# Block sums of x by VectorE out of PSUM, column tiles in the order 0, 3, 1, 4, 2, 5, and another first tile of seven products

## The chip, the cores and the metric

One core of a Trainium2 chip runs the whole program. The metric is the device time of one execution in microseconds (us). The kernel before was timed three times; the median counts.

## What is computed

Three layers follow each other: attention with a soft cap, a first feed-forward with a softmax-weighted unit and a layer norm, and a second feed-forward with a SiLU gate. All data are fp32.

```python
scores = cap * tanh(q @ k.T / sqrt(64) / cap)          # 2 batches, 12 heads, 448 positions, 64 wide
x = softmax(scores) @ v                                # 896 tokens, 768 wide
h = x @ w_in                                           # 768 -> 1024
e = exp(h - max(h)); solu = h * e / (sum(e) + 1e-9)
ln = (solu - mean) / sqrt(var + 1e-6) * g_ln
x = ln @ w_out                                         # 1024 -> 768: the "x" of this study
g = x @ w_gate                                         # 768 -> 1536
out = (g / (1 + exp(-g)) * (x @ w_val)) @ w_out2       # 1536 -> 768
```

## The kernel before, in words

Every fp32 product is made of three TensorE products of rounded parts: a number is split into `hi`, which ScalarE writes (`hi_act`, line 68), and `lo`, what is left, which VectorE subtracts (`lo_dve`, line 77). Each split so costs one ScalarE row and one VectorE row. The tiles read in the trace carry the names of the program: `x<-lA,wo` is a product of the layer-normed tokens with w_out, `g<-x,g` one of x with gate weights.

The second x is made transposed, in six column tiles `j` of 128 (`ff1_x2`, line 565), each for all 896 tokens. A tile is 384 tokens out of `lA` and 512 out of `lB`, eight fp32 steps each, in halves that alternate; the first two tiles have their last 512 tokens in two blocks of 256. Each block fills a PSUM bank; there are eight banks (tag "m"), handed out in turn. At the end of a block ScalarE and VectorE split the bank into `self.x2[j]`.

w_out arrives as 64-bit floats, 512 KB for half a tile (`load_w_out`, line 553). A half is turned into fp32 by one ScalarE row and four VectorE rows, scaled by g_ln in four ScalarE rows, and split by one row of either. So VectorE has ten rows of 512 numbers for each column tile besides the splits of x itself. TensorE needs the first half of w_out for the first half of a tile, and the second half for the second.

The second feed-forward takes w_gate and w_val in twelve column tiles `fc`. Tile 0 and tiles 7 to 11 are done directly (`ff2_gv`). Tiles 1 to 6 use seven block products in place of eight (`ff2_gv_seven`, line 677): gate and value of 128 columns, two halves of the 768 rows, two halves of the tokens. Four of the seven take block sums of x, the tensors T1 to T4; the others take x itself. The sums of weights S1 to S4 are made by `sum_steps` (line 646), S2 and S4 by one split into one tile.

The block sums of x are made while x runs. GpSimd adds `hi` and `lo` of a column tile back to fp32 (128x896) and subtracts blocks of 448 tokens (`x_sums`, line 628): 6 additions and 12 subtractions in the tile `xf`. During tile 0 of the second feed-forward `x_split` (line 640) splits the four sums of 1344 numbers into T, four ScalarE and four VectorE rows.

The rows of TensorE and of the attention stand in program order; ScalarE, VectorE and GpSimd rows of this part are put in order by a scheduler at build time, and each engine then runs its rows strictly in that order. DMAs are issued by SyncE; the raw weights have two buffers (tag "raw"), so a load starts when the last reader of the load before the last is done.

Of the kernel before, what the change touches and what calls it, by code (L numbers as in the profile page):

```python
# [5 lines left out]
F32 = mybir.dt.float32  # L6
# [4 lines left out]
AF = mybir.ActivationFunctionType  # L11
ALU = mybir.AluOpType
# [25 lines left out]
class Kernel:  # L38
# [526 lines left out]
    def ff1_x2(self, j, get, N, o):  # L565

        st = {}

        def part(a, z):
            def f():  # L570
                l, w = get(), self.wos[j]
                if a == 0:
                    st["ps"] = self.pt.tile([128, 512], F32, name=f"x2_{j}_{o}", tag="m")[:, :N]
                ps = st["ps"]
                for fc in range(a, z):
                    self.mm3(ps, (w[:, 0, fc, :], w[:, 1, fc, :]), (l[:, fc, 0, :], l[:, fc, 1, :]),
                             fc == 0, fc == self.K1 - 1)
                if z == self.K1:
                    hi, lo = self.x2[j][:, 0, o:o + N], self.x2[j][:, 1, o:o + N]
                    self.hi_act(hi, ps)  # L580
                    self.lo_dve(lo, ps, hi)
                    if o + N == 896 and j > 1:
                        for m in range(3) if j == 2 else (j,):
                            x = self.x2[m].bitcast(F32)
                            self.G.tensor_tensor(self.xf[:, m], x[:, 0], x[:, 1], op=ALU.add)
                        self.x_sums(j - 2)
            return (3 * (z - a) * N / 2400, f)

        c = self.K1 // 2
        return [part(0, c), part(c, self.K1)]  # L590
# [34 lines left out]
            self.V.tensor_tensor(self.S1f[:, k], self.S1f[:, k], sg[:, :self.HN], op=ALU.add)  # L625
        self.split((self.A22 if o else self.A11 if first else self.A12)[k], sg)

    def x_sums(self, i):

        c = i - 1  # L630
        x = [self.xf[:, k + 3 * (m // 2), 448 * (m % 2):448 * (m % 2) + 448] for m in range(4) for k in range(3)]
        x = [x[3 * m:3 * m + 3] for m in range(4)]
        if i == 0:
            todo = [(0, 1, 0, k) for k in range(3)]
        else:
            todo = [(1, 3, 1, c), (3, 3, 0, c), (2, 2, 3, c)]
        for d, p, m, k in todo:
            self.G.tensor_tensor(x[d][k], x[p][k], x[m][k], op=ALU.subtract)

    def x_split(self, i):  # L640

        d = (0, 3, 1, 2)[i]
        src = self.xf[:, 3 * (d // 2):3 * (d // 2) + 3, 448 * (d % 2):448 * (d % 2) + 448]
        self.split([self.T[i][:, u] for u in range(2)], src)

    def sum_steps(self, fc):

# [29 lines left out]
    def ff2_gv_seven(self, fc):  # L677

        V, add, mult = self.V, ALU.add, ALU.mult
        n, k, ee = self.HN, fc % self.KD, self.ee  # L680
        a, s24, s31, a22 = self.gvs[fc]
        half = lambda t, h: t.rearrange("p (h u k f) -> p h u k f", h=2, u=2, k=3)[:, h]
        A11, A12, S2, S4, S3, S1 = (half(t, h) for t in (a, s24, s31) for h in range(2))
        A22 = a22.rearrange("p u (k f) -> p u k f", k=3)
        X = lambda kh, th: [[self.x2[3 * kh + c][:, u, 448 * th:448 * th + 448] for u in range(2)] for c in range(3)]
        T1, T2, T3, T4 = ([[t[:, u, c] for u in range(2)] for c in range(3)] for t in self.T)
        bank = lambda m: self.pt.tile([128, 512], F32, name=f"{m}_{fc}", tag="m")[:, :448]

        def product(acc, w, x, start):
            for c in range(3):  # L690
                self.mm3(acc, (w[:, 0, c], w[:, 1, c]), x[c], start and c == 0, c == 2, not start)

        sg, c22, p1, u2 = (ee[:, 448 * m:448 * m + 448] for m in range(4))
        last = fc == self.KD
        first, second, third = (lambda: None,) * 3 if last else self.sum_steps(fc + 1)
        if last:
            self.load_gv(fc + 1, 1)
        a = bank("g")
        product(a, A11, X(0, 0), True)
        self.A.activation(p1, a, AF.Copy)  # L700
        b = bank("b")
        product(b, S2, T2, True)
        V.tensor_tensor(u2, p1, b, op=add)
        product(a, A12, X(1, 0), False)
        self.A.activation(sg, a, AF.Silu)
        first()
        product(b, S3, T3, False)
        V.tensor_tensor(p1, p1, b, op=add)
        c = bank("c")
        product(c, S1, T1, True)  # L710
        V.tensor_tensor(c22, p1, c, op=add)
        second()
        if last:
            self.load_gv(fc + 1, 0)
        e = bank("e")
        product(e, A22, T4, True)
        V.tensor_tensor(p1, p1, e, op=add)
        third()
        product(c, S4, X(1, 1), False)
        V.tensor_tensor(u2, u2, c, op=add)  # L720
        self.A.activation(u2, u2, AF.Silu)
        G = self.G
        if last:
            V.tensor_tensor(p1, p1, sg, op=mult)
            V.tensor_tensor(c22, c22, u2, op=mult)
            self.split(self.A12[k], p1[:, :n])
            V.tensor_tensor(self.S1f[:, k, :64], self.S1f[:, k, :64], p1[:, n:], op=add)
            V.tensor_tensor(self.S1f[:, k, 64:], self.S1f[:, k, 64:], c22[:, :320], op=add)
            for w, src in ((slice(0, 64), p1[:, n:]), (slice(64, 512), c22)):
                self.split([p[:, w] for p in self.A22[k]], src)  # L730
            return
        V.tensor_tensor(self.S3f[:, k], p1[:, :n], sg[:, :n], op=mult)
        V.tensor_tensor(self.S1f[:, k, :64], p1[:, n:], sg[:, n:], op=mult)
        self.split(self.A11[k], self.S3f[:, k])
        V.tensor_tensor(self.S1f[:, k, 64:], c22[:, :320], u2[:, :320], op=mult)
        G.tensor_tensor(c22[:, 320:], c22[:, 320:], u2[:, 320:], op=mult)
        G.tensor_tensor(self.S3f[:, k], self.S3f[:, k], self.S1f[:, k], op=ALU.subtract)
        self.split(self.A61[k], c22[:, 320:])
# [214 lines left out]
    def run(self):  # L953
        nc = self.nc
        KD, K1, K2, F1 = self.KD, self.K1, self.K2, self.F1
# [17 lines left out]
        f, g, hi, lo = zip(*w)  # L973
        self.w_steps = [((), f[0][:1], ()), (f[0][1:2], (), f[0][2:] + g[0][:1]), ((), (g[0][1], hi[0]), (lo[0],))]
        for i in range(1, KD):
            a = g[i][:1]
# [31 lines left out]
        lB = lp.tile([128, K1, 2, 512], F32R, name="lB", tag="lB")  # L1008
        T3, T4 = self.ff1_T(3, lambda: lB, 0), self.ff1_T(4, lambda: lB, 128)
        T5, T6 = self.ff1_T(5, lambda: lB, 256), self.ff1_T(6, lambda: lB, 384)  # L1010
        wo = [[(0.0, lambda j=j: self.load_w_out(j))] for j in range(KD)]
        lb = [lB[:, :, :, i * 256:(i + 1) * 256] for i in range(2)]
        blocks = ((lambda: lA, 384, 0), (lambda: lb[0], 256, 384), (lambda: lb[1], 256, 640))
        whole = (blocks[0], (lambda: lB, 512, 384))
        x2 = [[self.ff1_x2(j, *b) for b in (blocks if j < 2 else whole)] for j in range(KD)]

        steps = h[1] + h[2][:1] + T[0] + h[2][1:] + h[3][:1] + T[1] + h[3][1:] + wo[0] + h[4][:2] + T[2] + h[4][2:] + wo[1] + h[5][:5] + T3 + h[5][5:] + h[6][:-1] + T4 + h[6][-1:]
        for _, f in steps:
# [2 lines left out]
        n = self.HN = self.DM // 2  # L1021
        wb, gb = self.pool("wb"), self.pool("gb")
        self.g4 = [p.tile([128, 1536], F32R, name=f"g4_{i}", tag=f"g4_{i}") for i, p in enumerate((wb, wb, gb, gb))]
        self.xf = wb.tile([128, 6144], F32, name="xf", tag="w8")[:, :KD * 896].rearrange("p (k n) -> p k n", k=KD)
        X = self.slot("x", [128, KD, 2, 896], "x2")
        self.x2 = [X[:, j] for j in range(KD)]
        steps = x2[0][0] + x2[0][1] + wo[2] + x2[1][0][:1] + T5 + x2[1][0][1:] + x2[1][1] + T6
        steps += wo[3] + x2[2][0][:1] + x2[0][2] + x2[1][2]
        for j in range(2, KD):
            if 3 < j + 1 < KD:  # L1030
                steps += wo[j + 1]
            if j >= KD - 2:
                steps += [(0.0, lambda i=j - KD + 2: self.load_gv(0, i))]
            a, b = x2[j]
            steps += a[j == 2:1] + b[:1] + a[1:] + b[1:]
        for _, f in steps:
            f()
        self.wo.release()
# [22 lines left out]
        for fc in range(K2):  # L1061
# [8 lines left out]
            for i, (N, o) in enumerate(((n, 0), (512, n))):  # L1070
                if fc == 0:
                    if i == 0:
                        first, second, third = self.sum_steps(1)
                        first()
                        self.x_split(1)
                    else:
                        self.x_split(2)
                elif fc + 1 < K2:
                    self.load_gv(fc + 1, i)
                elif i == 0:  # L1080
                    self.load_w2(5)
                    self.load_w2(10)
                for c in early.get(fc, ())[i:i + 1]:
                    self.load_w2(c)
                self.ff2_gv(fc, N, o)
            if fc == 0:
                second()
                self.x_split(0)
                third()
                self.x_split(3)  # L1090

# [44 lines left out]
```

## Time and profile before

| | |
|---|---|
| median of 3 runs | 490.85 us (490.42 to 492.65) |
| the profiled execution: its time | 491.29 us |
| its span, from the first to the last instruction | 489.5 us |
| TensorE busy in the span | 474.3 us (97%) |
| VectorE, ScalarE, GpSimd busy | 392.7, 302.1, 77.9 us |
| mean granted TensorE clock | 0.99 of full speed |

The profile shows for each engine its rows: start, duration, engine, operation, the tiles written and read, shapes and a count of equal rows that follow each other. In brackets stands how long the engine stood idle before the row and whose work ended that. TensorE's matmul rows overlap: the next row starts before the one ahead has ended. A row of VectorE or ScalarE begins some 0.07 to 0.1 us before the row ahead ends, where it need not wait.

### The profile page before, as it was taken

How to read it: one execution, taken by the hardware profiler on the slowest of the kernel's cores; microseconds unless marked ns; L12 is line 12 of the kernel's file. 1: busy time of each engine (PE TensorE's matmuls, PEld its weight loads, DVE VectorE, ACT ScalarE, POOL GpSimd, SP SyncE). 2: the span in 40 equal slices, each digit the busy share in tenths (PEclk: the TensorE clock that was granted, in tenths of full speed). 3: DMA queues.
4: the chain of work that ended last, by engine and by line, in shares of the span. 5: the costliest groups of instructions: out<-in, count | busy, mean ns of one | idle time of the engine just before them, and what ended most of it. 6: DMA issues, size and time to landing. Idle time of an engine off the chain costs nothing.

```text
span 489.5 us, 7697 instructions
## 1 busy us (share of the span) xinstructions
PE 474.3 (97%) x2988; PEld 389.4 (80%) x2988; DVE 392.7 (80%) x635; ACT 302.1 (62%) x435; POOL 77.9 (16%) x102
## 2 busy tenths in 40 slices
PE   9999999999999999959979999999999999999997
PEld 7445454548888899848958999999888999999996
DVE  3689999887779989786897888888766756999991
ACT  5999999921324894356855666687868746335220
POOL 1020101040001004453742333310000000000000
PEclk9999999999999999988998999999999999999999
DMA  7777465002001222135414434335566741110012
GB/s 186 192 193 186 109 174 144 19 2 86 1 0 44 86 87 87 46 97 179 130 64 129 128 129 129 112 100 175 194 208 188 235 143 22 44 49 18 17 49 96
DMA packets 65060, 52.34 MB, mean 107 GB/s; under 512 B 35584, under 2 KB 61952, under 8 KB 64256
## 3 DMA queue, kind: packets, MB, share of 16 engines
q1 hardware_dynamic: 64992, 51.86, 35.5%
q8 instruction: 23, 0.38, 0.3%
q14 instruction: 13, 0.11, 0.1%
q0 software_dynamic: 32, 0.00, 0.0%
HBM read 49.10 MB, written 2.75 MB: 106 GB/s over the span
## 4 chain that ended last, share of the span: by engine, by line
PE 90%; DVE 6%; ACT 2%; issue 1%; DVEq 0%
PE p L30 16%; PE g L30 13%; PE h L30 12%; PE v L30 9%; PE pv L30 7%; PE sc L30 7%; PE x L30 6%; PE b L30 5%; PE c L30 5%; DVE wo L30 4%; PE S L30 4%; PE e L30 2%; PE lt L30 1%; ACT wo L30 1%; PE T L30 1%; PE warm L30 1%
## 5 line engine op out<-in xcount | busy, mean ns | idle before, releaser
L30 PE MATMUL g<-x,g 128*128 128x384 f32 (+2 forms) x324 | 69.8, 365 | 0.0
L30 PEld LDWEIGHTS g<-x,g 128*128 128x128 f32 x324 | 59.7, 188 | 6.5
L30 PE MATMUL h<-wi,x 128*128 128x512 f32 x252 | 59.2, 393 | 0.0
L30 PEld LDWEIGHTS h<-wi,x 128*128 128x128 f32 x252 | 46.8, 188 | 11.3 <-issue 1.5
L30 ACT ACTIVATE P<-sc,consts 112x896 f32<-112x896 f32 x48 | 45.4, 1010 | 3.7 <-PE sc L30 2.2
L30 PE MATMUL v<-x,g 128*128 128x384 f32 (+1 forms) x216 | 45.1, 362 | 0.0
L30 PEld LDWEIGHTS v<-x,g 128*128 128x128 f32 x216 | 39.1, 188 | 4.2
L30 ACT ACTIVATE P<-P,consts 112x3584 f32<-112x3584 f32 (+1 forms) x13 | 39.7, 3060 | 0.1
L30 PE MATMUL pv<-P,v 112*32 112x448 f32 x384 | 38.5, 540 | 0.0
L30 PEld LDWEIGHTS sc<-ks 64*112 64x112 f32 x288 | 23.3, 171 | 18.3 <-issue 7.7
L30 PE MATMUL x<-lA,wo 128*128 128x384 f32 x144 | 29.7, 355 | 6.6 <-DVE wo L30 6.0
L30 PE MATMUL sc<-ks 64*112 64x448 f32 x288 | 35.8, 379 | 0.2
L30 PE MATMUL x<-lB,wo 128*128 128x256 f32 (+1 forms) x192 | 35.4, 339 | 0.0
L30 PEld LDWEIGHTS x<-lA,wo 128*128 128x128 f32 x144 | 26.2, 198 | 8.6 <-DVE wo L30 7.1
L30 PEld LDWEIGHTS x<-lB,wo 128*128 128x128 f32 x192 | 30.0, 191 | 3.5
L30 PEld LDWEIGHTS pv<-P,v 112*32 112x32 f32 x384 | 12.2, 110 | 22.9 <-issue 20.9
L30 ACT ACTIVATE ee<-h,sms 128x512 f32<-128x512 f32 x14 | 9.5, 684 | 33.2 <-DVE sms L30 33.2
L30 PE MATMUL b<-a,g 128*128 128x448 f32 x108 | 25.9, 384 | 4.1 <-ACT g L30 3.8
L30 POOL COPY sm<-tr 32x14 f32<-32x14 f32 x48 | 14.8, 309 | 92.6 <-DVE tr L30 91.1
L30 ACT ACTIVATE wo<-wo,gt 128x128 f32<-128x128 f32 x48 | 15.3, 393 | 19.7 <-DVE wo L30 19.7
L30 PE MATMUL p<-w,a 128*128 128x384 f32 x144 | 26.7, 334 | 0.0
L30 PEld LDWEIGHTS b<-a,g 128*128 128x128 f32 x108 | 21.0, 197 | 7.0 <-ACT g L30 4.2
(203 smaller groups left out, 965.6 us busy)
## 6 DMA issues: line engine op xcount, KB each, us to landing
wg_raw<-in_moe_w_gate_dram SPq DMA_DIRECT2D x12, 765.8 KB, 4.2
wv_raw<-in_moe_w_val_dram SPq DMA_DIRECT2D x12, 765.8 KB, 4.2
wi_raw<-in_moe_w_in_dram SPq DMA_DIRECT2D x6, 1024.0 KB, 7.0
wo_raw<-in_moe_w_out_dram SPq DMA_DIRECT2D x12, 512.0 KB, 3.4
w_raw<-in_moe_w_out_dram SPq DMA_DIRECT2D x6, 767.6 KB, 4.3
v<-in_v_dram SPq DMA_DIRECT2D x24, 112.0 KB, 3.6
kq<-in_k_dram SPq DMA_DIRECT2D x22, 112.0 KB, 3.1
kq<-in_q_dram SPq DMA_DIRECT2D x22, 112.0 KB, 2.9
```

The lines of the kernel that those rows point to most:

```text
L30: i = f(*a, **k)
```

## The change

The six column tiles of x run in the order 0, 3, 1, 4, 2, 5, so that tiles `c` and `c + 3`, which the block sums combine, follow each other. `x_sums` moves from GpSimd to VectorE. It no longer adds `hi` and `lo` (except for the first 640 tokens of tiles 0 and 3), but subtracts straight out of the PSUM banks that hold x. No row takes two operands from PSUM: ScalarE copies one block of 448 tokens to SBUF for each of tiles 1 and 2. The sums have a layout of their own, in which each T is one piece.

```diff
-                    if o + N == 896 and j > 1:
-                        for m in range(3) if j == 2 else (j,):
-                            x = self.x2[m].bitcast(F32)
-                            self.G.tensor_tensor(self.xf[:, m], x[:, 0], x[:, 1], op=ALU.add)
-                        self.x_sums(j - 2)
+                    self.xps[j, o] = ps
...
-        for d, p, m, k in todo:
-            self.G.tensor_tensor(x[d][k], x[p][k], x[m][k], op=ALU.subtract)
+    def x_sub(self, t, c, a, z, p, m):
+
+        d = self.xf[:, t, c, a:z]
+        self.V.tensor_tensor(d, p, m, op=ALU.subtract)
+        return d
+
+    def x_sums0(self, j):
+
+        n, f = self.xps, self.xf[:, j // 3, 1:].rearrange("p c x -> p (c x)")[:, :640]
+        x = self.x2[j].bitcast(F32)
+        self.V.tensor_tensor(f, x[:, 0, :640], x[:, 1, :640], op=ALU.add)
+        t = lambda i: (self.xf[:, i, 0, :192], self.xf[:, i, 0, 192:])
+        if j == 0:
+            self.f0 = f
+            self.x_sub(0, 0, 0, 192, f[:, 448:], f[:, :192])
+            self.x_sub(0, 0, 192, 448, n[0, 640], f[:, 192:448])
+            return
+        self.x_sub(1, 0, 0, 192, f[:, 448:], t(0)[0])
+        self.x_sub(1, 0, 192, 448, n[3, 640], t(0)[1])
+        self.x_sub(3, 0, 0, 448, f[:, :448], self.xf[:, 1, 0])
+        self.x_sub(2, 0, 0, 448, self.xf[:, 1, 0], self.f0[:, :448])
+
+    def x_sums(self, j):
+
+        a, b, c, f = self.xps[j, 0], self.xps[j, 384], j % 3, self.x00
+        if j < 3:
+            self.A.activation(f[:, :384], a, AF.Copy)
+            self.A.activation(f[:, 384:], b[:, :64], AF.Copy)
+            self.x_sub(0, c, 0, 448, b[:, 64:], f)
+            return
+        t2 = self.x_sub(1, c, 0, 448, b[:, 64:], self.xf[:, 0, c])
+        self.x_sub(3, c, 0, 384, a, t2[:, :384])
+        self.x_sub(3, c, 384, 448, b[:, :64], t2[:, 384:])
+        self.x_sub(2, c, 0, 448, t2, f)
...
+        J = (0, 3, 1, 4, 2, 5)
```

In the first tile of seven products (`fc == 1`) the three products that take x itself come first: A11, then S4 in a bank of its own (`d`), then A12; the four with T follow. Since S4 and S1 are then in two banks, VectorE adds one row more. The splits of T0 come in the order of that use (`x_split` 1, 0, 2, 3).

```diff
         self.A.activation(p1, a, AF.Copy)
+        if fc == 1:
+            d = bank("d")
+            product(d, S4, X(1, 1), True)
+            product(a, A12, X(1, 0), False)
         b = bank("b")
         product(b, S2, T2, True)
         V.tensor_tensor(u2, p1, b, op=add)
-        product(a, A12, X(1, 0), False)
+        if fc == 1:
+            V.tensor_tensor(u2, u2, d, op=add)
+            c = bank("c")
+            product(c, S1, T1, True)
+        else:
+            product(a, A12, X(1, 0), False)
```

**Third column tile, ScalarE.** Here TensorE transposes the last tokens (`lt_0_2085`, `lt_1_2092`) and then begins the third column tile, whose weights are `wo_1988` (first half: `wo_0_1991`). Before, ScalarE's rows stood so:

```order
L30 ACTIVATE ee<-ee,sms 128x1024
L30 ACTIVATE wo_1988<-wo_0_1991 128x512
L30 ACTIVATE wo_1_2005<-wo_1_raw 128x512
L30 ACTIVATE x_1933<-x_1_384_2058 128x256
L30 ACTIVATE lB<-lt_0_2085 128x4x128
L30 ACTIVATE lB<-lt_1_2092 128x4x128
```

and now so:

```order
L30 ACTIVATE ee<-ee,sms 128x1024
L30 ACTIVATE wo_0_1991<-wo_0_1991,gt 128x128 x4
L30 ACTIVATE x_1933<-x_3_384_2058 128x256
L30 ACTIVATE lB<-lt_0_2085 128x4x128
L30 ACTIVATE wo_1988<-wo_0_1991 128x512
L30 ACTIVATE wo_1_2005<-wo_1_raw 128x512
L30 ACTIVATE lB<-lt_1_2092 128x4x128
```

The `hi` of the third tile's weights has moved behind two rows that wait for TensorE: the evacuation of the second tile's block and of the first four of the eight transposes.

**Fourth and fifth column tile, VectorE.** `x_4_0_2276` and `x_4_384_2289` are the banks of the fourth tile in the new order (column tile 4), `wo_2247` the weights of the fifth, `wo_1_2264` their second half. Now VectorE has:

```order
L30 TENSOR_TENSOR x_1933<-x_4_384_2289,x_1933 128x512
L30 TENSOR_TENSOR xf<-x_4_384_2289,xf 128x448
L30 TENSOR_TENSOR xf<-x_4_0_2276,xf 128x384
L30 TENSOR_TENSOR xf<-x_4_384_2289,xf 128x64
L30 TENSOR_TENSOR xf<-xf 128x448
L30 TENSOR_SCALAR wo_0_2337<-wo_0_2337 128x512
L30 TENSOR_TENSOR wo_2247<-wo_1_2264,wo_2247 128x512
```

where before, in the same place (column tile 3, weights `wo_2242`), it had:

```order
L30 TENSOR_TENSOR x_1933<-x_3_384_2284,x_1933 128x512
L30 TENSOR_SCALAR wo_0_2332<-wo_0_2332 128x512 x2
L30 SCALAR_TENSOR_TENSOR wo_0_2332<-wo_0_raw,wo_0_2332 128x512 x2
L30 TENSOR_TENSOR wo_2242<-wo_1_2259,wo_2242 128x512
```

Four sums stand ahead of the second half of the fifth tile's weights, and three conversion rows of the sixth have moved behind it.

**First tile of seven, TensorE.** `g_3_1931` is the weight tile that holds S2 and S4, `a_...` holds T, `x_1933` is x. Before:

```order
L30 MATMUL g_2635<-x_1933,g_0_1928 128x448 x9
L30 MATMUL b_2646<-a_2496,g_3_1931 128x448 x9
L30 MATMUL g_2635<-x_1933,g_0_1928 128x448 x9
L30 MATMUL b_2646<-a_2496,g_2_1930 128x448 x9
L30 MATMUL c_2683<-a_2496,g_2_1930 128x448 x9
```

Now:

```order
L30 MATMUL g_2639<-x_1933,g_0_1928 128x448 x9
L30 MATMUL d_2650<-x_1933,g_3_1931 128x448 x9
L30 MATMUL g_2639<-x_1933,g_0_1928 128x448 x9
L30 MATMUL b_2669<-a_2500,g_3_1931 128x448 x9
L30 MATMUL c_2681<-a_2500,g_2_1930 128x448 x9
```

The second product takes x where it took T, but its weights are still in `g_3_1931`.

## Rows read from the trace of the kernel before

**Rows 1.** The page: the chain that ended last, by engine.
```profile
PE 90%; DVE 6%; ACT 2%; issue 1%; DVEq 0%
```

**Rows 2.** Busy time and granted clock in stretches of the span (us).
```profile
core 0: us, PE busy (x) PEld busy (x) DVE busy (x) ACT busy (x) POOL busy (x), PEclk, DMA share, GB/s
188.90:219.90 31.00, 25.18 (x128) 21.52 (x126) 26.74 (x26) 13.50 (x35) 17.11 (x10) 0.95 0.24 72
...
257.30:262.00 4.70, 4.38 (x14) 3.63 (x15) 2.63 (x5) 3.22 (x5) 0.00 (x0) 0.64 0.36 109
```

**Rows 3.** TensorE in order of time: start, us, row, [idle before, what ended it].
```profile
182.79 2.35 PE L30 MATMUL x<-lA,wo 128*128 128x384 f32 x12
...
198.34 2.27 PE L30 MATMUL x<-lA,wo 128*128 128x384 f32 x12
...
208.74 2.73 PE L30 MATMUL x<-lA,wo 128*128 128x384 f32 x12 [0.51 <-ACT wo L30]
...
219.86 3.57 PE L30 MATMUL x<-lA,wo 128*128 128x384 f32 x10 [5.21 <-DVE wo L30]
...
232.39 2.01 PE L30 MATMUL x<-lA,wo 128*128 128x384 f32 x10 [0.80 <-DVE wo L30]
...
257.28 0.68 PE L30 MATMUL b<-a,g 128*128 128x448 f32 x2 [3.83 <-ACT g L30]
258.28 2.98 PE L30 MATMUL b<-a,g 128*128 128x448 f32 x7 [0.32 <-DVE g L30]
...
263.02 2.02 PE L30 MATMUL b<-a,g 128*128 128x448 f32 x9
```

**Rows 4.** VectorE by shape from 160 to 188 us: count, busy us, mean ns.
```profile
L30 DVE SCALAR_TENSOR_TENSOR wo<-wo_raw,wo 128x512 uint32<-128x512 uint32 x12 | 8.2, 686 | 0.1
...
L30 DVE TENSOR_TENSOR wo<-wo,wo 128x512 fp32r<-128x512 f32 x4 | 2.7, 686 | 1.1 <-ACT wo L30 1.1
...
L30 DVE TENSOR_SCALAR wo<-wo 128x512 uint32<-128x512 uint32 x5 | 2.1, 421 | 0.1
```

**Rows 5.** VectorE by shape from 188.9 to 220 us.
```profile
L30 DVE SCALAR_TENSOR_TENSOR wo<-wo_raw,wo 128x512 uint32<-128x512 uint32 x8 | 10.6, 1325 | 0.2
L30 DVE TENSOR_TENSOR wo<-wo,wo 128x512 fp32r<-128x512 f32 x5 | 7.2, 1460 | 2.1 <-ACT wo L30 2.0
L30 DVE TENSOR_SCALAR wo<-wo 128x512 uint32<-128x512 uint32 x4 | 5.3, 1324 | 0.1
...
L30 DVE TENSOR_TENSOR x<-x,x 128x512 fp32r<-128x512 f32 x2 | 1.4, 683 | 0.0
```

**Rows 6.** VectorE by shape from 237.5 to 257 us.
```profile
L30 DVE TENSOR_TENSOR a<-xf,a 128x1344 fp32r<-128x1344 f32 x4 | 9.2, 2303 | 0.5 <-ACT a L30 0.5
L30 DVE SCALAR_TENSOR_TENSOR wv<-wv_raw,wv 128x768 uint32<-128x768 uint32 x1 | 1.9, 1910 | 0.0
L30 DVE TENSOR_TENSOR g<-wg,g 128x768 fp32r<-128x768 f32 x1 | 1.9, 1909 | 0.0
L30 DVE TENSOR_TENSOR w<-wv,w 128x384 fp32r<-128x384 f32 x1 | 1.5, 1510 | 0.0
L30 DVE SCALAR_TENSOR_TENSOR wg<-wg_raw,wg 128x768 uint32<-128x768 uint32 x1 | 1.0, 951 | 0.0
...
L30 DVE TENSOR_TENSOR wg<-t,wg 128x384 f32<-128x384 f32 x1 | 0.5, 545 | 0.0
```

**Rows 7.** ScalarE in order of time, at the start of the third column tile.
```profile
182.63 1.09 ACT L30 ACTIVATE lB<-lt 128x512 fp32r<-128x512 f32 x2
```

**Rows 8.** GpSimd by shape from 188 to 252 us.
```profile
L30 POOL TENSOR_TENSOR xf<-xf 128x448 f32<-128x448 f32 x12 | 19.8, 1654 | 0.9
...
L30 POOL TENSOR_TENSOR wv<-wg,wv 128x384 f32<-128x384 f32 x1 | 1.3, 1335 | 0.0
L30 POOL TENSOR_TENSOR t<-wv 128x384 f32<-128x384 f32 x1 | 1.0, 1016 | 1.0 <-DVE wv L30 1.0
```

**Rows 9.** SyncE in order of time: the issue of the first w_val load.
```profile
225.94 0.37 SPq L155 DMA_DIRECT2D wv_raw<-in_moe_w_val_dram  x1
```

More of the change, by code (lines that the diff above doesn't have):

```diff
@@ L626, in ff2_gv @@
         self.split((self.A22 if o else self.A11 if first else self.A12)[k], sg)
[L628 to L636, printed above, removed]
-        for d, p, m, k in todo:
-            self.G.tensor_tensor(x[d][k], x[p][k], x[m][k], op=ALU.subtract)
+    def x_sub(self, t, c, a, z, p, m):
[27 more added lines that the diff above has]
+        self.x_sub(2, c, 0, 448, t2, f)
     def x_split(self, i):
-        d = (0, 3, 1, 2)[i]
-        src = self.xf[:, 3 * (d // 2):3 * (d // 2) + 3, 448 * (d % 2):448 * (d % 2) + 448]
-        self.split([self.T[i][:, u] for u in range(2)], src)
+        self.split([self.T[i][:, u] for u in range(2)], self.xf[:, i])
     def sum_steps(self, fc):
@@ L708, in ff2_gv_seven @@
         V.tensor_tensor(p1, p1, b, op=add)
-        c = bank("c")
-        product(c, S1, T1, True)
+        if fc > 1:
+            c = bank("c")
+            product(c, S1, T1, True)
         V.tensor_tensor(c22, p1, c, op=add)
@@ L718, in ff2_gv_seven @@
         third()
-        product(c, S4, X(1, 1), False)
+        if fc > 1:
+            product(c, S4, X(1, 1), False)
         V.tensor_tensor(u2, u2, c, op=add)
@@ L1010, in run @@
         T5, T6 = self.ff1_T(5, lambda: lB, 256), self.ff1_T(6, lambda: lB, 384)
-        wo = [[(0.0, lambda j=j: self.load_w_out(j))] for j in range(KD)]
+        J = (0, 3, 1, 4, 2, 5)
+        wo = [[(0.0, lambda j=j: self.load_w_out(j))] for j in J]
         lb = [lB[:, :, :, i * 256:(i + 1) * 256] for i in range(2)]
@@ L1014, in run @@
         whole = (blocks[0], (lambda: lB, 512, 384))
-        x2 = [[self.ff1_x2(j, *b) for b in (blocks if j < 2 else whole)] for j in range(KD)]
+        x2 = [[self.ff1_x2(j, *b) for b in (blocks if i < 2 else whole)] for i, j in enumerate(J)]
         steps = h[1] + h[2][:1] + T[0] + h[2][1:] + h[3][:1] + T[1] + h[3][1:] + wo[0] + h[4][:2] + T[2] + h[4][2:] + wo[1] + h[5][:5] + T3 + h[5][5:] + h[6][:-1] + T4 + h[6][-1:]
@@ L1023, in run @@
         self.g4 = [p.tile([128, 1536], F32R, name=f"g4_{i}", tag=f"g4_{i}") for i, p in enumerate((wb, wb, gb, gb))]
-        self.xf = wb.tile([128, 6144], F32, name="xf", tag="w8")[:, :KD * 896].rearrange("p (k n) -> p k n", k=KD)
+        self.xf = wb.tile([128, 6144], F32, name="xf", tag="w8")
+        self.xf, self.x00 = self.xf[:, :5376].rearrange("p (t c n) -> p t c n", t=4, c=3), self.xf[:, 5376:5824]
+        self.xps = {}
         X = self.slot("x", [128, KD, 2, 896], "x2")
@@ L1027, in run @@
         steps = x2[0][0] + x2[0][1] + wo[2] + x2[1][0][:1] + T5 + x2[1][0][1:] + x2[1][1] + T6
-        steps += wo[3] + x2[2][0][:1] + x2[0][2] + x2[1][2]
+        steps += wo[3] + x2[2][0][:1] + x2[0][2] + x2[1][2] + [(0.0, lambda j=j: self.x_sums0(j)) for j in J[:2]]
         for j in range(2, KD):
@@ L1034, in run @@
             a, b = x2[j]
-            steps += a[j == 2:1] + b[:1] + a[1:] + b[1:]
+            steps += a[j == 2:1] + b[:1] + a[1:] + b[1:] + [(0.0, lambda j=J[j]: self.x_sums(j))]
         for _, f in steps:
@@ L1076, in run @@
                     else:
-                        self.x_split(2)
+                        self.x_split(0)
                 elif fc + 1 < K2:
@@ L1087, in run @@
                 second()
-                self.x_split(0)
+                self.x_split(2)
                 third()
```

## The prediction

> **What bounds the kernel now.** I read the chain that ended last, then TensorE in order of time where the chain leaves it, then the queue of the engine that TensorE waits for. The chain is TensorE for 90% of the span [rows 1], so time is only to be had where TensorE stands still. It does so in one region, from the making of x (about 167 to 237 us) to the first tile of seven products (to 262 us): 0.51, 5.21, 0.80, 3.83 and 0.32 us, in all 10.67 us [rows 3]. The first three are waits for weights of w_out, the last two for the weight tile with S2 and S4. The row at 208.74 took 2.73 us where its like at 198.34 took 2.27, so 0.46 us more is hidden inside it. And the clock falls after the two long waits: 0.95 in the mean of 188.9 to 219.9 us and 0.64 from 257.3 to 262 [rows 2], that is, part of these stretches ran at 1.2 in place of 2.4 GHz. The rows behind the waits show its price: ten matmuls of 384 in 3.57 us, where twelve take 2.27 and ten so about 1.92, is 1.65 lost; seven of 448 in 2.98, where nine take 2.02 and seven so about 1.61, is 1.37 lost [rows 3]. Together the region loses 10.67 + 0.46 + 3.02 = 14.15 us. The profiled execution took 491.29 us; without these losses it would take **477.1 us**. The changed kernel is that plus the waits it has.
>
> Why are the weights late? VectorE's rows on w_out stretch from 188.9 us on, when GpSimd begins its sums (17.1 us busy in 31, [rows 2]). From 160 to 188 the three shapes take 0.686, 0.686 and 0.421 us [rows 4]; from 188.9 to 220 they take 1.325, 1.460 and 1.324 [rows 5]. That is 10.6 - 8 x 0.686 = 5.1, 7.2 - 5 x 0.686 = 3.8 and 5.3 - 4 x 0.421 = 3.6 us, **12.5 us of VectorE's time in 31**. Rows that take x from PSUM aren't stretched (0.683 for 512 [rows 5]). From 237.5 to 257 the same is seen: four T splits take 9.2 us where, drawn from 0.545 for 384 and 0.951 for 768, each would take 1.56: 3.0 lost; three more rows lose 0.96 each, 5.9 us in all [rows 6].
>
> **The change, part by part.**
>
> *GpSimd's 18 rows go, and with them the stretching.* So I take the waits of 0.51, 5.21 and 0.46 us as gone, and the clock's 1.65 behind them. VectorE's own load for one column tile allows it: ten weight rows, 2 x (2 x 0.421 + 3 x 0.686) = 5.8 us less 0.7 of overlap, and two rows of x of 1.2, so 6.3 us, where TensorE takes 9.9 us for a tile (from 198.34 to 208.23, when it stood free [rows 3]).
>
> *VectorE gets 19 rows.* Priced from the shapes above less 0.07 us of overlap: two of 640 numbers at 0.75 (between 0.686 for 512 [rows 4] and 0.951 for 768 [rows 6]), two of 192 at 0.27, two of 256 at 0.34, eight of 448 at 0.54, two of 384 at 0.47, two of 64 at 0.14: 8.3 us, and one addition of 448 in the first tile of seven, 0.54. The trace has no subtraction of this kind out of PSUM; the nearest is the `lo` of x, 0.683 for 512 [rows 5], equal to 0.686 from SBUF [rows 4], so I take no surcharge; the upper bound is the stretched 1.46. In the tile with most of it this makes 6.3 + 1.7 = 8.0 us, still under 9.9.
>
> *Where these rows stand ahead of weights.* Behind the fourth tile VectorE has its last x split, four sums and a conversion row before it comes to the second half of the fifth tile's weights: 0.2 + 0.6 (ScalarE's `hi`) + 0.6 + 1.7 + 0.4 + 0.6 = 4.1 us after TensorE ends the tile, and TensorE wants it after half a tile, 4.9 us. So nothing is lost, with 0.8 us to spare; upper bound 1 us.
>
> *Third tile, a new wait.* ScalarE's `hi` of its weights now stands behind the first four transposes' evacuation. That one begins at 182.63 and takes about 0.6 [rows 7]; the weights' `hi` then ends at about 183.75. VectorE's `lo` stands behind the `lo` of the transposes and the sum of 640: 183.2 + 0.6 + 0.75 + 0.7 = 185.25. TensorE is there at 182.85, and began without a wait before (182.79, [rows 3]). It loses 0.9 us to `hi` and, after two matmuls, 1.2 to `lo`: **2.1 us** (1.5 to 2.6; the whole count hangs on TensorE's own progress, so it moves with it).
>
> *Sixth tile.* The same weights were 0.80 us late before [rows 3]. ScalarE has two copies more in that queue (384 and 64 numbers, about 0.4 and 0.1 us by the 0.55 for 512 in [rows 7]), VectorE one sum of 0.54, part of it beside ScalarE's. I add 0.5: **1.3 us** (0.5 to 2).
>
> *First tile of seven.* Its second product now takes x and not T, but S4's weights, which lie in the same tile as S2's. It was these that TensorE waited for, 3.83 + 0.32 us [rows 3], not T. So the reordering gives nothing by itself. What counts is when VectorE gets to S2/S4. It is spared the 5.9 us of [rows 6], of which I leave 0.4, since two GpSimd rows of 1.02 and 1.33 us stay [rows 8]. It has 1.7 us of sums of the sixth tile more. And it starts later against TensorE: x ends 0.51 + 5.21 + 0.46 + 0.80 + 1.65 - 2.1 - 1.3 = 5.2 us earlier, but the weights that ScalarE converts ahead of x's last split hang on the first w_val load, issued at 225.94 [rows 9] when VectorE has freed a raw buffer. That row follows the fifth tile's last split: 208.23 + 2.1 + 9.9 + 0.2 + 0.6 + 0.6 + 1.4 (two rows of 0.686) gives about 222.5 to 223, some 3.4 us earlier, so 1.8 are lost. 4.15 - 5.5 + 1.7 + 1.8 = **2.1 us** (0.5 to 4.15). The page SBUF — State Buffer of the Trainium skill (Who interferes with whom) says that GpSimd and a VectorE instruction with two SBUF inputs exclude each other for a whole instruction. By that rule the two rows that stay could cost up to 2.35 us in place of my 0.4, and the wait would be 4.1; the trace agrees with the rule's form, since only rows without a PSUM input are stretched [rows 5], but no row shows that both will meet.
>
> *Second tile of seven.* Its first bank must be copied by ScalarE before the third product adds to it. ScalarE's order there has a conversion row and a split of 128 more ahead of that copy, and VectorE the extra addition of 0.54. Priced between nothing and one product (2.02 us [rows 3]): **1.0 us**.
>
> *Clock.* After waits of 5.21 and 3.83 us it fell, after 0.80 not. Waits of 2.1 lie between, so I take one fall at 1.37 us, **1.4** (0 to 4 falls).
>
> Sum: 477.1 + 2.1 + 1.3 + 2.1 + 1.0 + 1.4 = 485.0 us against 491.29 for the profiled execution. The median of the runs lies 0.44 below that, so **484.6 us**, 1.3% less.
>
> **Rivals.**
> - *More is won.* S2/S4 come in time and no wait brings the clock down. For it: the 5.9 us VectorE is spared there exceed the wait. Against: x's last split is tied to the w_val load. Price: 2.1 + 1.4 + half of the 1.0 less, 480.6 us.
> - *No change: each of the short waits brings the clock down.* Four falls at 1.37 to 1.65 in place of one, 4 x 1.5 - 1.4 = 4.6 us more: 489.2. For it: both waits above 3 us did this. Against: the 0.80 did not, and the four lie 8 us or more apart with TensorE busy between.
> - *Slower: the stretching isn't GpSimd's doing* (the loads or the bank reads, say) *and stays.* Then the 8.3 us of sums come on top of a VectorE that already decides the x part: 490.85 + 8.3 = 499.2 us. It decides from about 8 of the 14.15 us staying, when the sums eat what is left. Against: rows of one shape are short before 188.9 us, with loads running in both stretches.
>
> **How the numbers follow.** My forecast 0.74 (its own range 482 to 488), more won 0.12, no change 0.09, slower 0.05. A change of this kernel is told from none at about 0.5%, 2.45 us: below 488.4 is faster. Forecast and "more won" fall there: 0.86; the clock rival is the same: 0.09; slower 0.05. The lower bounds of the waits give 477.1 + 1.5 + 0.5 + 0.5 - 0.4 = 479.2, the upper without the clock 477.1 + 2.6 + 1 + 2 + 4.15 + 2 - 0.4 = 488.5. The range leaves out a tenth at either end: 481.4 to 488.4.
>
> **What would show it.** No VectorE row of w_out above 0.75 us; no wait of TensorE in the fourth to fifth tile; waits near 2 us for `wo` at the third tile and 1.3 at the sixth; the product `d` waiting about 2 us for ScalarE's or VectorE's `g`; x ending about 5 us earlier. I am wrong if VectorE's rows stay long, if sums out of PSUM take more than 0.8 us, or if the clock is low for more than about 3 us of the region.

## The result and the profile after

The changed kernel takes **485.21 us** (median of 4 runs, 483.92 to 486.31), the kernel before beside it 490.63 (490.22 to 492.65): a ratio of 0.988, 95% interval 0.9844 to 0.9917. The forecast was 484.6. The profiled execution took 485.31 us, with a span of 483.5.

The chain that ended last, by engine, against [rows 1]:
```profile
PE 91%; DVE 4%; ACT 2%; issue 1%; DMA 1%; POOL 0%; ACTq 0%; SPq 0%
```
TensorE in order of time, from the third column tile to the second tile of seven products, against [rows 3]:
```profile
183.91 0.61 PE L30 MATMUL x<-lA,wo 128*128 128x384 f32 x2 [0.77 <-ACT wo L30]
185.45 2.86 PE L30 MATMUL x<-lA,wo 128*128 128x384 f32 x10 [0.93 <-DVE wo L30]
188.11 9.37 PE L30 MATMUL x<-lB,wo 128*128 128x256 f32 x60
...
211.91 2.27 PE L30 MATMUL x<-lA,wo 128*128 128x384 f32 x12
...
216.78 2.27 PE L30 MATMUL x<-lA,wo 128*128 128x384 f32 x12
...
227.12 0.61 PE L30 MATMUL x<-lA,wo 128*128 128x384 f32 x2 [0.44 <-ACT wo L30]
228.19 2.03 PE L30 MATMUL x<-lA,wo 128*128 128x384 f32 x10 [0.47 <-DVE wo L30]
...
232.82 3.31 PE L30 MATMUL g<-x,g 128*128 128x384 f32 x18
...
251.28 0.68 PE L30 MATMUL d<-x,g 128*128 128x448 f32 x2 [2.00 <-ACT g L30]
252.27 1.68 PE L30 MATMUL d<-x,g 128*128 128x448 f32 x7 [0.31 <-DVE g L30]
...
268.10 2.12 PE L30 MATMUL g<-x,g 128*128 128x448 f32 x9 [1.38 <-ACT ee L30]
```
The waits of 0.51 and 5.21 us in the fifth tile and the slow row at its start [rows 3] are gone: its halves start at 211.91 and 216.78 without a wait. In their place stand small ones: 0.77 + 0.93 at the third tile, 0.44 + 0.47 at the sixth, 2.00 + 0.31 in the first tile of seven, 1.38 in the second. The ten matmuls at 185.45 take 2.86 us where ten took about 1.92, and the 60 behind them 9.37 where they take 8.66 when nothing disturbs (E8 below): 0.94 + 0.71 = 1.65 us, counted as the prediction counts. Ten that start behind the same two waits with the clock up take 2.03 (E2, at 186.47), so about 1.5 us of it are the clock's. The granted clock shows the same place, and GpSimd without work there, against [rows 2]:
```profile
184.50:192.50 8.00, 7.07 (x42) 7.05 (x42) 5.79 (x13) 2.98 (x8) 0.00 (x0) 0.79 0.28 78
```
From 188.9 to 219.9 us, where it was busy for 17.11 us [rows 2], GpSimd has no row at all.

VectorE by shape from 188.9 to 219.9 us (count, busy us, mean ns), against [rows 5]:
```profile
L30 DVE SCALAR_TENSOR_TENSOR wo<-wo_raw,wo 128x512 uint32<-128x512 uint32 x10 | 6.9, 690 | 0.3
L30 DVE TENSOR_TENSOR wo<-wo,wo 128x512 fp32r<-128x512 f32 x5 | 3.4, 688 | 4.5 <-ACT wo L30 4.5
L30 DVE TENSOR_TENSOR xf<-xf 128x448 f32<-128x448 f32 x3 | 1.8, 617 | 0.0
...
L30 DVE TENSOR_SCALAR wo<-wo 128x512 uint32<-128x512 uint32 x4 | 1.7, 421 | 0.0
```
The rows that took 1325, 1460 and 1324 ns are back at 690, 688 and 421. Further on, two GpSimd rows are left, and there VectorE still stretches:
```profile
242.46 3.85 DVE L30 TENSOR_TENSOR a<-xf,a 128x1344 fp32r<-128x1344 f32 x2
246.23 1.36 DVE L30 TENSOR_TENSOR a<-ee,a 128x384 fp32r<-128x384 f32 x1
```
```profile
242.62 2.28 POOL L30 TENSOR_TENSOR t<-wv 128x384 f32<-128x384 f32 x1 [64.17 <-DVE wv L30]
244.97 2.21 POOL L30 TENSOR_TENSOR wv<-wg,wv 128x384 f32<-128x384 f32 x1
```
The first fence is VectorE in order of time, the second GpSimd. Without a GpSimd row beside them the three splits take 3.03 and 0.55 us (E7 below), so VectorE loses 0.82 + 0.81 = 1.63 us. The GpSimd rows take 2.28 and 2.21 where one alone takes 1.02 (at 255.61; 1.016 in [rows 8]).

### The profile page after: what moved, and what is told of

The parts are those of the page before. It is cut to its first block, busy times and chain, and to the rows that moved or that the text cites. A ratio compares the mean times of both kernels' runs of the same rounds, so it can differ in the third digit from the quotient of the medians.

```text
span 483.5 us, 7699 instructions
## 1 busy us (share of the span) xinstructions
PE 472.7 (98%) x2988; PEld 388.3 (80%) x2988; DVE 382.4 (79%) x654; ACT 303.0 (63%) x439; POOL 47.0 (10%) x84
## 4 chain that ended last, share of the span: by engine, by line
PE 91%; DVE 4%; ACT 2%; issue 1%; DMA 1%; POOL 0%; ACTq 0%; SPq 0%
PE p L30 16%; PE h L30 12%; PE g L30 11%; PE x L30 10%; PE pv L30 8%; PE v L30 7%; PE sc L30 7%; PE S L30 4%; PE c L30 4%; PE b L30 4%; PE e L30 2%; PE lt L30 1%; DVE a L30 1%; PE T L30 1%; PE warm L30 1%
## 5 line engine op out<-in xcount | busy, mean ns | idle before, releaser
L30 PE MATMUL x<-lA,wo 128*128 128x384 f32 x144 | 28.7, 348 | 2.6 <-DVE wo L30 1.4
L30 PEld LDWEIGHTS p<-w,a 128*128 128x128 f32 x144 | 25.2, 188 | 0.1
L30 PE MATMUL b<-a,g 128*128 128x448 f32 x108 | 24.1, 367 | 0.0
L30 DVE TENSOR_TENSOR g<-wg,g 128x768 fp32r<-128x768 f32 x18 | 17.9, 993 | 6.6 <-ACT g L30 6.6
```

The source lines that it names most:

```text
L30: i = f(*a, **k)
```

## The experiments

The runs of the kernel before that stood beside them had medians of 490.0 to 490.5 us. Where a ratio is given, it is to those.

**E1: the order of products as before**, in all tiles (each condition stands twice):
```
-        if fc == 1:
+        if fc == 0:
...
-        if fc > 1:
+        if fc > 0:
```

> The changed kernel with the products of the first tile of seven in the order of before (A11, S2 with T2, A12, ...), all else as changed. Theory 'GpSimd' (the gain is that GpSimd's sums no longer stretch VectorE's rows, and the new product order gives nothing because S2 and S4 lie in one tile): the wait of about 2.3 us before the second product stays, the time stays at 485.2 us within 1. Rival 'T': the gain of that tile comes from taking the products without T first: the wait goes back to about 4.2 us, 487 us or more.

483.62 us (483.31 to 485.47), 0.9876 (0.9828 to 0.9923). The profile (TensorE in order of time):
```profile
250.92 0.68 PE L30 MATMUL b<-a,g 128*128 128x448 f32 x2 [2.15 <-ACT g L30]
```
With the 0.32 us behind these two matmuls the wait is 2.47 in place of 2.31, and no wait follows in the second tile. So in these profiles the new order of products wins nothing; it brings the 1.38 us. A second pair is E13.

**E2: GpSimd works again, on data that nobody reads.** After each group of sums, five additions of 320 numbers; everything else is as in the changed kernel.
```
+    def dead_sums(self, j):
+        x, d = self.x2[j].bitcast(F32), self.dead
+        for m in range(5):
+            self.G.tensor_tensor(d, x[:, 0, 144 * m:144 * m + 320], x[:, 1, 144 * m:144 * m + 320], op=ALU.add)
```


> The changed kernel with GpSimd kept busy as before: 30 additions of 128x320, five behind each column tile of x, into a part of a tile that nobody reads; the result is not changed by them. VectorE's and ScalarE's order is that of the changed kernel. Theory 'GpSimd': rows of VectorE with both inputs in SBUF stretch again (512 numbers from 0.69 to above 1.2 us), rows out of PSUM do not, waits for weights of w_out come back from the fourth tile on, and the time is 488 to 494 us. Rival 'stretching has another cause' (the loads, the banks): the time stays at 485.2 within 1.

497.01 us (494.14 to 497.71), 1.013 (1.0076 to 1.0184): more than I expected. GpSimd is about as busy as before (16.27 us from 188.9 to 219.9, against 17.11 [rows 2]), and VectorE has the sums on top; so it comes near the 499.2 us at which the prediction priced stretching that stays. VectorE by shape from 188.9 to 219.9 us, then TensorE in order of time:
```profile
L30 DVE SCALAR_TENSOR_TENSOR wo<-wo_raw,wo 128x512 uint32<-128x512 uint32 x9 | 8.5, 950 | 0.2
L30 DVE TENSOR_TENSOR wo<-wo,wo 128x512 fp32r<-128x512 f32 x5 | 5.0, 995 | 4.1 <-ACT wo L30 4.1
...
L30 DVE TENSOR_SCALAR wo<-wo 128x512 f32<-128x512 f32 x4 | 3.1, 765 | 0.0
...
L30 DVE TENSOR_TENSOR x<-x,x 128x512 fp32r<-128x512 f32 x2 | 1.4, 682 | 0.0
L30 DVE TENSOR_TENSOR xf<-x,xf 128x448 f32<-128x448 f32 x2 | 1.2, 618 | 0.3 <-ACT xf L30 0.3
```
```profile
221.25 3.57 PE L30 MATMUL x<-lA,wo 128*128 128x384 f32 x10 [2.73 <-DVE wo L30]
...
263.03 3.97 PE L30 MATMUL d<-x,g 128*128 128x448 f32 x9 [3.68 <-ACT g L30]
```
No transfer was added and no engine waits for the added rows (the two sums of weights that remain on GpSimd started after it had stood idle for 2.90 us, so these rows did not delay them); yet the stretched rows and the long waits are back. That the stretching is GpSimd's doing is shown. The two last VectorE rows read x from PSUM and keep their 682 and 618 ns.

**E3: the engine alone.** The kernel before, with its 18 sums on VectorE; column order, products and sums stay.
```
-                            self.G.tensor_tensor(self.xf[:, m], x[:, 0], x[:, 1], op=ALU.add)
+                            self.V.tensor_tensor(self.xf[:, m], x[:, 0], x[:, 1], op=ALU.add)
...
-            self.G.tensor_tensor(x[d][k], x[p][k], x[m][k], op=ALU.subtract)
+            self.V.tensor_tensor(x[d][k], x[p][k], x[m][k], op=ALU.subtract)
```

> The kernel before with the 18 sums moved to VectorE as they are (hi and lo added to fp32, then subtracted; column order, layout and products of before). VectorE gets 6 rows of 896 at about 1.0 and 12 of 448 at 0.54, 12.5 us, in place of the change's 8.3. Theory 'GpSimd': the engine is what counts; no row is stretched, VectorE has 6.3 + 2.6 us in a tile of 9.9, and the time is 485 to 488 us. Rival 'order': the pairs of column tiles and the reading out of PSUM are needed, and VectorE's longer queue eats the gain: 489.5 or more.

484.4 us (484.37 to 484.49), 0.9884 (0.984 to 0.9928). TensorE in order of time:
```profile
214.51 0.62 PE L30 MATMUL x<-lA,wo 128*128 128x384 f32 x2 [0.72 <-ACT wo L30]
...
227.51 3.92 PE L30 MATMUL x<-lA,wo 128*128 128x384 f32 x12 [2.53 <-ACT wo L30]
...
252.01 0.67 PE L30 MATMUL b<-a,g 128*128 128x448 f32 x2 [1.17 <-ACT g L30]
254.13 1.68 PE L30 MATMUL b<-a,g 128*128 128x448 f32 x7 [1.45 <-DVE g L30]
```
The whole gain is there, a little more than I expected. The waits stand elsewhere (fifth and sixth tile in place of third and sixth, one fall of the clock in the sixth), and the product `b` waits 2.62 us.

**E4: the column order alone.** The kernel before with the tiles in order 0, 3, 1, 4, 2, 5, and its sums grouped by that order, still on GpSimd.
```
...
-        wo = [[(0.0, lambda j=j: self.load_w_out(j))] for j in range(KD)]
+        J = (0, 3, 1, 4, 2, 5)
+        wo = [[(0.0, lambda j=j: self.load_w_out(j))] for j in J]
...
```


> The kernel before with the column order 0, 3, 1, 4, 2, 5 alone; the sums stay on GpSimd, four subtractions in a burst behind each pair. Theory 'GpSimd': no gain, 489 to 493 us, VectorE's rows stretched as before. Rival 'order': the pairing itself helps, since fewer sums are left behind the last tile: 488.5 or less.

490.3 us (488.38 to 491.39, 10 runs), 0.9999 (0.9975 to 1.0022), with the wait of [rows 3] unchanged:
```profile
219.28 3.49 PE L30 MATMUL x<-lA,wo 128*128 128x384 f32 x10 [5.21 <-DVE wo L30]
```

**E6: the A12 product ahead of S4's, in a bank of its own** (on the changed kernel):
```
+            a2 = bank("h")
+            product(a2, A12, X(1, 0), True)
+            V.tensor_tensor(sg, p1, a2, op=add)
             product(d, S4, X(1, 1), True)
-            product(a, A12, X(1, 0), False)
...
-        self.A.activation(sg, a, AF.Silu)
+        self.A.activation(sg, sg if fc == 1 else a, AF.Silu)
```


> The changed kernel with, in the first tile of seven, A12 ahead of S4 and in a bank of its own, so that it needs neither T nor S4 nor the copy of the first bank; VectorE has one addition more. Theory 'weights' (TensorE waits there for the tile with S2 and S4, 2.3 us): A12 fills 1.86 us of it, the wait falls to about 0.5 and the time by about 1.9, to 483.3 us. Rival: the wait moves on to the next products, since VectorE is late as a whole: within 0.7 of 485.2.

481.83 us (480.62 to 484.49), 0.9822 (0.9776 to 0.9867). TensorE:
```profile
250.87 0.67 PE L30 MATMUL d<-x,g 128*128 128x448 f32 x2 [0.17 <-ACT g L30]
```
`d` waits 0.17 + 0.32 in place of 2.00 + 0.31: 1.82 us, near the 1.86 of the theory. The profiled span is 3.0 shorter; 1.2 of that is another thing and is told under the hardware.

**E7: the two remaining sums of weights on VectorE** (on the changed kernel).
```
-        S = self.G
+        S = self.V if fc == 1 else self.G
```

> The changed kernel with the two sums of weights for the first tile of seven (128x384 each, s1 and v - s1's partner) on VectorE in place of GpSimd. On GpSimd they took 2.28 and 2.21 us and VectorE's T splits beside them lost 1.6 us. Theory 'GpSimd': VectorE spends 0.95 us more and loses 1.6 less, S4 comes about 0.7 us earlier, 484.5 us. Rival: VectorE's queue is the bound and the added rows cost what they take: 486.2 us.

485.76 us (485.09 to 486.72), 0.9896 (0.986 to 0.9932): no gain. The stretching goes (first fence, VectorE), the wait grows (second fence, TensorE), and a load comes late (third fence, ScalarE):
```profile
242.76 3.03 DVE L30 TENSOR_TENSOR a<-xf,a 128x1344 fp32r<-128x1344 f32 x2
...
246.18 0.55 DVE L30 TENSOR_TENSOR a<-ee,a 128x384 fp32r<-128x384 f32 x1
```
```profile
251.77 0.68 PE L30 MATMUL d<-x,g 128*128 128x448 f32 x2 [2.93 <-ACT g L30]
```
```profile
231.42 0.98 ACT L30 ACTIVATE wg<-wg_raw,consts 128x768 f32<-128x768 int8 x1 [0.97 <-DMA wg_raw<-in_moe_w_gate_dram]
```
Two rows of 0.55 come onto VectorE for the 1.63 saved, which leaves 0.5; and the order around them moves: ScalarE now has a split of 128 and an evacuation of 448 numbers ahead of the conversion of `wg`. The weights are ready 20.4 us after x ends, before 19.45. But part of that is not the edit's. The load of w_gate was converted 6.47 us after its issue (224.95), and ScalarE waited 0.97 for it; in the changed kernel it was there after 5.71 at most, without a wait. VectorE's T splits began 0.30 us later for it, although x ended 0.44 earlier. Then the clock falls as well. So this profile does not price the edit by itself.

**E8: the two sums of 640 numbers held behind the blocks of the first two tiles**, and so behind the third tile's weights, in program order (on the changed kernel):
```
+        self.in_order = True
         self.V.tensor_tensor(f, x[:, 0, :640], x[:, 1, :640], op=ALU.add)
+        self.in_order = False
```


> The changed kernel with the two additions of 640 numbers held behind the blocks of the first two tiles, which gives ScalarE and VectorE the order of before around the third tile. Theory 'order at the third tile': its waits of 0.77 and 0.93 us go, and the low clock behind them (1.65 us) with them: 482 to 483.5 us. Rival: the waits come back a tile later, since the sums only move: within 0.7 of 485.2.

483.16 us (483.04 to 484.55), 0.985 (0.9807 to 0.9892). TensorE in order of time:
```profile
182.77 2.35 PE L30 MATMUL x<-lA,wo 128*128 128x384 f32 x12
184.97 8.66 PE L30 MATMUL x<-lB,wo 128*128 128x256 f32 x60
...
214.03 2.01 PE L30 MATMUL x<-lA,wo 128*128 128x384 f32 x10 [0.58 <-DVE wo L30]
...
228.55 3.31 PE L30 MATMUL g<-x,g 128*128 128x384 f32 x18
...
248.11 3.97 PE L30 MATMUL d<-x,g 128*128 128x448 f32 x9 [3.10 <-ACT g L30]
251.88 3.12 PE L30 MATMUL g<-x,g 128*128 128x448 f32 x9
```
The waits of the third and sixth tile and the fall of the clock are gone; one of 0.58 us has come into the fifth. That is the rival in part, but x ends 4.27 us earlier. Then the 2.00 us ahead of `d` become 3.10, and the clock falls there: that row and the next take 3.97 and 3.12 us where nine matmuls take 1.99. Most of what was won is given back: the third product of the second tile starts 0.96 us earlier than in the changed kernel (267.14 against 268.10), and the rest of the 2.1 us in the profiled span is the pace told under the hardware.

**E9: E6, E7 and E8 together.**

> The three edits together: A12 ahead of S4 in a bank of its own, the first weight sums on VectorE, the additions of 640 held back. If the three waits are independent the gains add up: 1.9 + 0.7 + 2.5 or more, 479 to 481.5 us. If they are one queue (VectorE late as a whole) the sum is less: 482 or more.

480.16 us (479.04 to 483.23), 0.979 (0.9743 to 0.9837). With A12's product as cover, the clock stays up (granted 1.00 from 237 to 262), and `d` waits 1.41 + 0.45. Most of what E8 won is kept here: x ends 4.20 us before E6's, and the third product of the second tile starts 3.10 before E6's. The time is in the range of "the gains add up", but not by the gains that I added: the medians give 3.4 for E6, 2.05 for E8 and nothing for E7. No run has E6 and E8 without E7, so what E7's rows do in this one is not shown.

**E10 and E11: the old order of products with E6's cover and E8's sum; E11 with E7's rows too.** The diff is those of E1, E6 and E8 (E11: and E7), with A12's product ahead of S2's.

> Sums on VectorE and the new column order as in the change; the order of the seven products as before, except that the product of A12 runs ahead of S2's in a bank of its own; the sum of 640 numbers held behind the third column tile's weights. Theory (the reordered products bring the wait of 1.4 us in the second tile of seven and take none away; S2's and S4's weights are ready 19.5 us after x ends, whatever stands ahead, as long as the two remaining sums of weights stay on GpSimd): x ends at 228.4, the weights are ready at 247.9, TensorE is free at 246.7, so it waits 1.2, and not at all in the second tile of seven; against the run with all three edits that is 2.1 us less, 478 us (477 to 479.5). Rival (the reordering hides something in the first tile that comes back when it is undone): a wait of 2.5 us or more there, 480 or more.

> The same, with the first two sums of weights on VectorE as well. Theory (the two rows and what moves ahead with them in VectorE's and ScalarE's order make the weights 1 us later, more than the stretching that goes): 0.6 to 1 us slower than the run beside it, 478.9 us, TensorE waiting about 2 us in the first tile of seven. Rival (the two GpSimd rows cost VectorE 1.6 us, and with them gone the weights come earlier): 477.3, with a wait under 0.7 us.

E10: 483.22 us (480.81 to 484.95, 6 runs), 0.9854 (0.9822 to 0.9886). E11: 480.66 (479.43 to 482.34, 6 runs), 0.9813 (0.9783 to 0.9842). Both of my theories fell. TensorE in E10:
```profile
249.36 0.67 PE L30 MATMUL b<-a,g 128*128 128x448 f32 x2 [2.10 <-ACT g L30]
250.60 1.69 PE L30 MATMUL b<-a,g 128*128 128x448 f32 x7 [0.57 <-DVE g L30]
253.00 2.08 PE L30 MATMUL b<-a,g 128*128 128x448 f32 x9 [0.71 <-DVE ee L30]
```
The weights are ready 21.6 us after x ends, not 19.5. ScalarE in order of time shows why:
```profile
247.23 0.92 ACT L30 ACTIVATE wg<-wg,consts 128x768 int32<-128x768 f32 x1
248.06 0.52 ACT L30 ACTIVATE ee<-g 128x448 f32<-128x448 f32 x1
248.48 1.60 ACT L30 ACTIVATE g<-wg 128x768 fp32r<-128x768 f32 x2
```
The first two rows, and a split of 128 ahead of them, now stand before the split of S2 and S4 (the third row, with the split behind it); in the changed kernel they stand behind it (it starts at 250.40, they follow from 251.13). So ScalarE's part of the split starts 19.5 us after x ends and not 17.6. VectorE's addition from A12's bank and a conversion row, ahead of its own part, add the difference of 0.57 and 0.31 us. And with A12's product moved forward, nothing stands between S2's product and S3's in the same bank, which VectorE must first have read: 0.71 us, a cover that I had not counted. In E11's profile these waits sum to 3.09, in E10's to 3.38. So the weight sums on VectorE cost nothing that these two show, while E7 showed no gain; the intervals of E10 and E11 overlap, and which engine is better for them stays open.

**E12 and E13: the changed kernel and E1 once more, side by side.**

> The changed kernel once more, beside the one with the old order of products. 485.2 us (484 to 486.3). Its profile also tells whether the time of a product of nine matmuls (1.82 or 1.86 us from start to start, with TensorE busy) is the kernel's or the execution's: if the kernel's, 1.86 again from 270 us on; if the execution's, either.

> The changed kernel with the order of the seven products as before, once more. Theory (the reordering costs the wait of 1.38 us in the second tile and gives 0.16 in the first): 1.2 us under the run of the changed kernel beside it, 484.0. Rival (the difference of 1.6 us seen so far was chance): within 0.5 us of it.

E12: 484.04 us (483.08 to 485.93, 6 runs), 0.9883 (0.9855 to 0.9911). E13: 482.71 (482.04 to 486.58, 6 runs), 0.9859 (0.9826 to 0.9893). The old order is 1.3 us ahead, after 1.6 in the first pair, where 1.2 was worked out from the waits. Each pair's intervals overlap, so I take it as likely: the new order of products costs about 1.3 us.

## Why the prediction was right, point by point

**The stretching is GpSimd's** (the step on which everything hangs): right, shown by E2 and E3. The rival by which it stays, 499.2 us, falls. That VectorE has room for the sums and that PSUM adds no surcharge is right: 617 to 618 ns for 448 numbers, from SBUF and from PSUM alike. I had priced 540 net of overlap.

The page SBUF — State Buffer of the Trainium skill (Who interferes with whom) has GpSimd share one pair of ports with VectorE, held for a whole instruction, and used by VectorE for a second SBUF input or in a two-port mode. The traces agree: rows with one input from PSUM stay at 682 and 618 ns beside GpSimd, and of the rows with a single SBUF input it is the fast ones (417 to 422 ns for 512 numbers alone) that stretch, to 765 in E2 and 1324 in [rows 5].

**Fourth and fifth tile**: no wait, as forecast.

**Third tile**: forecast 2.1 us (0.9 + 1.2), measured 0.77 + 0.93 = 1.70, behind the rows that were named. E8, where the sum of 640 is held back and both engines have the order of before, has neither wait; so that order is the cause.

**Sixth tile**: 1.3 forecast, 0.91 measured. That these weights are late in themselves is not shown: E8 has no wait there and one of 0.58 in the fifth tile.

**First tile of seven**: 2.1 forecast, 2.31 measured, and that was luck: three terms were mis-sized and cancel. First, I left 0.4 us for the two GpSimd rows that stay. They did meet VectorE's splits and cost 1.63. The rule that the prediction cites from the Trainium skill (SBUF — State Buffer, Who interferes with whom) had put it at up to 2.35, and was the nearer one. Second, x ended 4.2 us earlier (237.00 to 232.82) and not 5.2, because the clock fell in the third tile (1.65) while the waits there and in the sixth were 0.8 shorter than forecast; and the w_val load's issue came at 224.56, against 222.5 to 223; ScalarE then waited 2.02 us for its landing. So 4.2 - 1.4 = 2.8 us were lost there, where I had 1.8. Third, VectorE was spared more than the window of [rows 6] shows, since its rows ahead of it were stretched too. In the kernel before:
```profile
228.96 1.82 DVE L30 TENSOR_TENSOR g<-wg,g 128x768 fp32r<-128x768 f32 x1 [1.21 <-ACT g L30]
230.70 1.64 DVE L30 TENSOR_TENSOR wo<-wo,wo 128x512 fp32r<-128x512 f32 x1
232.80 1.37 DVE L30 SCALAR_TENSOR_TENSOR wv<-wv_raw,wv 128x768 uint32<-128x768 uint32 x1 [0.46 <-ACT wv L30]
```
Their like take 0.96, 0.68 and 0.96 in the changed kernel, 2.2 us less. With these three put in, the sum is 4.15 - (5.9 + 2.2 - 1.63) + 1.7 + 2.8 = 2.2. It stays an estimate: it counts rows of one queue, and a load that lands late (E7, E13) moves the wait by a microsecond. That the reordered products would give nothing was right.

**Second tile of seven**: 1.0 forecast, 1.38 measured. E1 has none of it.

**Clock**: one fall was forecast, 1.4 us, for waits of about 2 us. One came, 1.65 us, but behind shorter waits, at the third tile. E12, the same kernel, has both (granted 0.79 from 184.5 to 192.5 us, 0.72 from 251 to 257). So I had the size of a fall and not its place, that there was just one is this execution's, and the argument from waits above 3 us was wrong: two waits of 0.77 and 0.93 near each other were enough here, and in five of the six other profiles that have them.

The sum of the losses is 1.70 + 0.91 + 2.31 + 1.38 + 1.65 = 7.95 us, where 7.9 was forecast: 477.1 + 7.95 = 485.05, measured 485.31. The terms were each off by up to 0.4, in both directions; that the sum comes within 0.3 us is in part luck. The rival "more is won" (480.6) needed the waits and falls covered; E9 and E11 reach its time with other edits, E9 by such cover. The rival of four falls (489.2) didn't come about.

**Which part does it**: the engine (E3: 484.4). The column order alone does nothing (E4), and with VectorE it only moves the waits. The order of products likely costs 1.3 us.

## What to carry to other kernels

Before giving GpSimd a sum because it is idle, look at what VectorE does beside it: here its rows with two inputs from SBUF waited for GpSimd and were waited for, its fast rows (421 ns for 512 numbers) waited too, and moving 18 rows onto the busier engine won 1.2% (E3). When weights are made just in time, an earlier arrival of TensorE can lengthen the next wait, and a wait can bring the clock down (both in E8): give it a product that needs nothing new as cover, and check what that product covered where it stood. A row that nobody waits for should be held behind the ones that somebody does.

## What the runs showed of the hardware

**The same product runs at two paces.** With TensorE busy and the granted clock at 1.00, a product of nine matmuls of 448 starts 1.86 us after the one before in some stretches and 1.83 in others, for tens of products on end. The changed kernel, then E12, which is the same kernel:
```profile
273.77 2.02 PE L30 MATMUL e<-a,w 128*128 128x448 f32 x9
275.63 2.02 PE L30 MATMUL c<-x,g 128*128 128x448 f32 x9
```
```profile
274.83 1.99 PE L30 MATMUL e<-a,w 128*128 128x448 f32 x9
276.66 1.99 PE L30 MATMUL c<-x,g 128*128 128x448 f32 x9
```
It is thus the execution's, not the kernel's; where it changed in these profiles, it did so at a wait. From the third product of the second tile to the end, the changed kernel's profile takes 210.8 us and those of E12, E6 and E8 209.6: 1.2 us, which is what E6's span won beyond its 1.82. What sets it stays open.

**Executions of one kernel differ by a transfer.** E13's profiled execution took 486.58 us, E1's, the same kernel, 483.61. ScalarE in order of time, in E1 and in E13:
```profile
230.73 1.00 ACT L30 ACTIVATE wg<-wg_raw,consts 128x768 f32<-128x768 int8 x1 [0.17 <-DMA wg_raw<-in_moe_w_gate_dram]
```
```profile
232.16 0.99 ACT L30 ACTIVATE wg<-wg_raw,consts 128x768 f32<-128x768 int8 x1 [1.31 <-DMA wg_raw<-in_moe_w_gate_dram]
```
The load was issued at 224.88 and 225.22, and ScalarE had it 5.85 and 6.94 us after that, 1.1 later in E13; TensorE then waited 3.26 us and not 2.15 for the first weights of seven, and behind that the clock fell: seven matmuls took 2.30 us and not 1.71, the nine after them 3.00 and not 2.02. Of the 3.0 us between the two, the wait is 1.1 and the clock 1.5; 0.3 was there when x ended.

**A fall of the clock costs nearly the same each time at one place, and not at another.** At the third tile six profiles have it (the changed kernel, E1, E6, E7, E12, E13): from the ten matmuls behind the waits to the row after the 60 that follow them, 11.86 to 11.89 us pass. E2, with waits of 0.77 and 0.92 in the same place, had no fall, and there it is 10.36. So the fall costs 1.5 us, and the waits alone don't tell whether it comes. At `d` it varies: from its start to that of the second product behind it, 4.33 us pass in the changed kernel, where the clock stays up, and 5.41 in E12, 5.91 in E7 and 6.73 in E8, where it falls.
